# One scan and a reciprocal in place of two scans in a chunked linear-attention kernel

## The chip, the cores and the metric

The kernel runs on one core of a Trainium2 chip. A core has TensorE (PE, matrix products, with a queue of its own for loading weights, PEld), VectorE (DVE), ScalarE (ACT), GpSimd (POOL) and SyncE (SP, which here only issues DMAs). The metric is the device time of one execution in microseconds; the median over the runs counts.

## The reference

The reference is a linear attention with a decay for each channel, followed by a mixture of experts. Batch 4, 8 heads, 768 tokens, head size 48; 8 experts, model width 384, hidden width 1024.

```python
for t in range(S):
    kt, vt, rt, wt = (k[:, :, t], v[:, :, t], r[:, :, t], w[:, :, t])
    cur = np.einsum('bhd,bhe->bhde', u[None] * kt, vt)
    y[:, :, t] = np.einsum('bhd,bhde->bhe', rt, state + cur)
    state = wt[:, :, :, None] * state + np.einsum('bhd,bhe->bhde', kt, vt)
...
skip_score = x @ w_skip
do_compute = skip_score > 0
out = x.copy()
xc = x[do_compute]
e_idx = np.argmax(xc @ w_gate, axis=1)
...
    h = np.maximum(xc[mask] @ w1[e], 0.0)
    y[mask] = gate_w[mask, None] * (h @ w2[e])
out[do_compute] = xc + y
```

The decay `w` lies between 0.8 and 0.95 here. Everything is float32.

## The kernel before

**Chunks.** The 768 tokens of a batch are cut into 6 chunks of 128 tokens, so there are 24 chunks, `i` = 0 to 23. Channels lie on the partitions: two heads of 48 channels at partitions 0 and 64, four such pairs (`NP` = 4) side by side in the free dimension. A tile of one chunk is thus 128 partitions by 4 x 128 numbers. `wrk` holds `w` (4 rows of 129, `CW`, the last column a zero between pairs), `r` and `k` of a chunk.

**What is made of the decays.** `prep_scan` (L277) runs a scan over `w` backwards: `q[j]` is the product of the decays from token `j` to the end of the chunk, started anew at each pair by the `floor` operand, which lies in the PSUM tile `pss`. `prep_keys` takes the reciprocal `rq` of `q[0]`, one number for each pair (L284), forms `kq = k * q[j+1]` on POOL (L287), and runs a second scan, forwards, that gives `rh[j]`, the product of the decays before token `j` (L289). `prep_reads` forms `rp = r * rq * rh` with four operations of DVE, one for each pair (L297), and `rk = r * k` on POOL (L302). `beside` ties POOL's operation to the last of the four `rp`, so that it starts after them. With `kq` and `rp`, PE computes the scores inside a chunk (L328, `psA`), transposes `kq` (L321), and multiplies `rp` with the state (L383).

**The loop.** The order of all work is written out by hand. A pass `s` of the attention loop issues the loads of chunk `s+4`, stores chunk `s-1`, updates and carries the state of chunk `s`, scans chunk `s+2`, forms the outputs of chunk `s` (L378 and L383, into the PSUM tile `psY`), prepares keys and reads of chunk `s+2`, and computes scores, the two masks `asb` (L334) and the bonus (L343, L347) of chunk `s+1`. On DVE the order in a pass is: scan, `rq`, scan, four `rp`, two masks, bonus. The bonus writes `psY`, on which L378 then accumulates. Three `wrk` buffers go round: the load of a chunk waits until POOL's `rk` and ACT's check (L311) of the chunk three before have read theirs. SP issues its DMAs in order.

**The router.** After every sixth chunk a generator `router` computes which expert each token goes to; it yields after each small step, and `drip` issues one, two or four of these steps at fixed places in the pass: before the scan, between `prep_keys` and `prep_reads`, and after the bonus. They run on DVE (shown as L205, a helper's line), some on ACT and POOL, and PE writes its results into `pss`, the same tile in which `floor` lies. Up to two `mark` steps of two ACT operations each come in a pass.

**Weights during attention.** With `k = s - 3`, the first weights are fetched during the attention loop: `load_weights(e, q)` yields after each of three DMAs of 512 KB (L90); `q` = 0 is the first matrix, `q` = 1 the second. They go to two raw buffers: the first matrix of expert 0 to one, the other three in turn to the second. The pass then casts slices of 512 columns to a high part on ACT (`split_slice`, L107); the low part, raw minus high, is put on the list `lows` and taken by POOL in the next pass, beside the scan (L273).

**After attention.** The rest of the router for the last chunks, the first expert's first half on PE meanwhile (L126, L582), then the stage of the experts with gathered tokens (L768 to L795).

Of the kernel before, what the change touches and what calls it, by code (L numbers as in the profile page):

```python
# [8 lines left out]
F32 = mybir.dt.float32  # L9
# [5 lines left out]
ALU = mybir.AluOpType  # L15
# [5 lines left out]
P = 128  # L21
# [5 lines left out]
NP = H // 2  # L27
# [3 lines left out]
CW = P + 1  # L31
# [4 lines left out]
HEAD = 6  # L36
STEP = 214
W_AT = 4
Q_MIN = 1e-30
RW = 1 + NP * CW + 3 * NP * P + 3  # L40
R_OFF = 1 + NP * CW
# [15 lines left out]
def rwkv_moe_kernel(ctx, tc, wrk, wrk0, vN, uP, wgs, wgp, w12, cst, out):  # L57
    nc = tc.nc
# [12 lines left out]
    def beside(ins, op):  # L71
        tc.add_manual_dep(ins.ins, op.ins.name,
                          mybir.DependencyInfo(mybir.DependencyClass.Sync,
                                               mybir.DependencyReason.DATA),
                          reason="shared port")
    WN = ("w1h", "w1l", "w2h", "w2l")

    def wtile(e, k):
        nm = f"{WN[k]}{e % 2}"
        pool = wset0 if nm in ("w1h1", "w1l1", "w2h0", "w2l0") else wset1[0]  # L80
        t = wsp[e, k] = pool.tile([P, KC * DF], F32R, tag=nm, name=f"{nm}_{e}")
        return t
# [11 lines left out]
    def split(dst_h, dst_l, src, eng=None):  # L94
        nc.scalar.copy(dst_h, src)
        (eng or nc.vector).tensor_tensor(dst_l, src, dst_h.bitcast(F32), op=ALU.subtract)

    def split_slice(e, i, eng=None):
        q, cs = i // 6, slice((i % 6) * 512, (i % 6 + 1) * 512)
        for k in (2 * q, 2 * q + 1):  # L100
            if (e, k) not in wsp:
                wtile(e, k)
        hi, lo, raw = wsp[e, 2 * q][:, cs], wsp[e, 2 * q + 1][:, cs], raws[e, q][:, cs]
        if eng is None:
            split(hi, lo, raw)
        else:
            nc.scalar.copy(hi, raw)  # L107
            lows.append((lo, raw, hi.bitcast(F32)))
# [24 lines left out]
    with tc.tile_pool(name="att", bufs=2) as att, \  # L133
# [6 lines left out]
        def load_chunk(i):  # L140
            b, c = seq[i]
            t = wrk_sb[i % NBUF]
            vf = vt_sb[i % (NBUF + 1)].rearrange("p a j -> p (a j)")
            if i == 0:
                nc.sync.dma_start(t[:, :R_OFF], wrk0[:, :R_OFF])
                nc.scalar.dma_start(t[:, K_OFF:V_OFF], wrk0[:, K_OFF:V_OFF])
                nc.sync.dma_start(t[:, R_OFF:K_OFF], wrk0[:, R_OFF:K_OFF])
                nc.scalar.dma_start(c_sb[:, :C_IOTA], cst[:, :C_IOTA])
                nc.sync.dma_start(u_sb, uP)
                nc.scalar.dma_start(vf, wrk0[:, V_OFF:V_OFF + NP * P])  # L150
                return
            for g in range(2):
                nc.sync.dma_start(t[64 * g:64 * g + D], wrk[b, c, g, :, :V_OFF])
            for g in range(2):
                nc.sync.dma_start(vf[64 * g:64 * g + D], wrk[b, c, g, :, V_OFF:V_OFF + NP * P])

        def load_v(i):
            b, c = seq[i]
            v_sb[i] = att.tile([P, H, D], F32, tag="v", name=f"v{i}", bufs=4)
            nc.sync.dma_start(v_sb[i], vN[b, c])  # L160
# [36 lines left out]
        floor = pss[:, 200:200 + NP * CW // 2].bitcast(BF16)  # L197
        pt = pss[:, 64:64 + 2 * NV * E].rearrange("p (j q e) -> p j q e", j=2, q=NV)

        class Steps:  # L200
            last = None
# [9 lines left out]
        def setup():  # L211
# [5 lines left out]
            nc.vector.memset(bias_hi, -Q_MAX)  # L217
            nc.vector.memset(smask, Q_MIN)
            nc.vector.memset(smask[:, :, 0:1], 1.0)
# [32 lines left out]
        def flush():  # L252
            while held:
                held.pop(0)()

        def drip(k=1):
            for _ in range(k):
                while later and next(later[0], None) is None:
                    later.popleft()
# [20 lines left out]

        def prep_keys(i):
            wk = work[i]
            rq = wk["rq"] = att.tile([P, NP, 1], F32, tag="rq", name=f"rq{i}")
            nc.vector.reciprocal(rq, wk["q"][:, :, 0:1])  # L284

            kq = wk["kq"] = att.tile([P, NP, P], F32, tag="kq", name=f"kq{i}")
            nc.gpsimd.tensor_tensor(kq, wk["k"], wk["q"][:, :, 1:CW], op=ALU.mult)  # L287
            rh = wk["rh"] = att.tile([P, NP, CW], F32, tag="rh", name=f"rh{i}", bufs=1)
            nc.vector.tensor_tensor_scan(  # L289
                rh.rearrange("p a j -> p (a j)"), wk["w"][:, 0:NP * CW], floor, 0.0,  # L290
                op0=ALU.mult, op1=ALU.max)

        def prep_reads(i):
            wk = work[i]
            rp = wk["rp"] = att.tile([P, NP, P], F32, tag="rp", name=f"rp{i}", bufs=3)
            for a in range(NP):
                last = nc.vector.scalar_tensor_tensor(  # L297
                    rp[:, a], wk["r"][:, a], wk["rq"][:, a], wk["rh"][:, a, :P],
                    op0=ALU.mult, op1=ALU.mult)

            rk = wk["rk"] = att.tile([P, NP, P], F32, tag="rk", name=f"rk{i}")
            mul = nc.gpsimd.tensor_tensor(rk.rearrange("p a j -> p (a j)"),  # L302
                                          wk["w"][:, R_OFF:K_OFF], wk["w"][:, K_OFF:V_OFF],
                                          op=ALU.mult)
            beside(mul, last)
# [281 lines left out]
        def fill(k):  # L587
            psw = ps1.tile([P, 512], F32, tag="psT", name="psw", bufs=2)
            for _ in range(k):
                nc.tensor.matmul(psw, warm[:, :P], warm, start=True, stop=True)  # L590

        with tc.manual_schedule():
            setup()
            fill(FILL0)
            for s in range(-2, n + 1):
                on = lambda i: 0 <= i < n
                if s + 4 < n:
                    load_chunk(s + 4)
                if on(s + 3) and s + 3 >= 1:
                    load_v(s + 3)  # L600
                if s == -2:
                    nc.sync.dma_start(c_sb[:, C_IOTA:], cst[:, C_IOTA:])
                    nc.sync.dma_start(wgp_sb[:, 0::2], wgp[:, 0::2])
                    nc.sync.dma_start(wgp_sb[:, 1::2, E + 1:], wgp[:, 1::2, :2 * D])
                    nc.sync.dma_start(wgp_sb[:, 1::2, :E + 1], wgp[:, 1::2, 2 * D:])
                if s == -1:
                    nc.sync.dma_start(wgs_sb, wgs)
                if on(s - 1):
                    store(s - 1)
                for i0, m in GROUPS:  # L610
                    if i0 + m == s:
                        pace[0] = 1 if i0 + m < LATE else 2
                        later.append(router(i0, m))
                        if i0 + m == LATE:
                            later.append(early())
                if on(s):
                    update(s)
                    carry(s)
                drip(pace[0])
                if on(s + 2):  # L620
                    prep_scan(s + 2)
                if on(s):
                    outputs(s)
                flush()
                if on(s + 2):
                    prep_keys(s + 2)
                    drip(2 * pace[0])
                    prep_reads(s + 2)
                if on(s):
                    evict(s)  # L630
                if on(s + 1):
                    intra(s + 1)
                    mask(s + 1, 0)
                    mask(s + 1, 1)
                    bonus_sums(s + 1)
                    bonus(s + 1)
                    drip(2 * pace[0])
                if on(s + 2):
                    prep_check(s + 2)
                for _ in range(min(2, len(marks))):  # L640
                    marks.popleft()()
                if s == n - 1:
                    early_tokens(0)
                if on(s):
                    rows_out(s)
                flush()
                if s == -2:
                    nc.vector.tensor_copy(trib, tri)
                    nc.gpsimd.tensor_copy(identb, ident)
                    nc.gpsimd.tensor_copy(iota, c_sb[:, C_IOTA:C_IOTA + 2 * P])  # L650
                k = s + 1 - W_AT
                for eq, k0 in (((0, 1), 0), ((0, 0), 3), ((1, 0), 8), ((1, 1), 16)):
                    if k == k0:
                        gens[eq] = load_weights(*eq)
                    if k0 <= k < k0 + 3:
                        next(gens[eq])
                if 1 <= k < 7:
                    split_slice(0, 5 + k, nc.gpsimd)
                if 9 <= k < 15:
                    split_slice(1, k - 9, nc.gpsimd)  # L660

        while len(later) > 1:
            drip()
# [308 lines left out]
```

## Time and profile before

| | |
|---|---|
| median of 3 runs | 317.33 us (316.35 to 317.79) |
| profiled execution | 317.5 us, of which 315.6 us is the span |
| busy share of the span | PE 93%, PEld 85%, DVE 78%, ACT 59%, POOL 37% |
| scan `q` (L277), 24 times | 29.1 us in all |
| scan `rh` (L289), 24 times | 28.9 us |
| `rp` (L297), 96 times | 33.1 us |
| `kq` and `rk` on POOL, 24 times each | 28.6 and 30.6 us |

The span runs from the first to the last instruction. The attention loop fills about the first half of it; the experts fill the second. Shares are means over both, so the stages have to be looked at by themselves. In rows of the order of time the first number is the start, the second the duration of the group, and brackets hold the idle time of the engine before it and what ended it. Operations of one engine overlap a little at their ends, so that a queue of them advances by somewhat less than the sum of their durations.

### The profile page before, as it was taken

How to read it: one execution, taken by the hardware profiler on the slowest of the kernel's cores; microseconds unless marked ns; L12 is line 12 of the kernel's file. 1: busy time of each engine (PE TensorE's matmuls, PEld its weight loads, DVE VectorE, ACT ScalarE, POOL GpSimd, SP SyncE). 2: the span in 40 equal slices, each digit the busy share in tenths (PEclk: the TensorE clock that was granted, in tenths of full speed). 3: DMA queues.
4: the chain of work that ended last, by engine and by line, in shares of the span. 5: the costliest groups of instructions: out<-in, count | busy, mean ns of one | idle time of the engine just before them, and what ended most of it. 6: DMA issues, size and time to landing. Idle time of an engine off the chain costs nothing.

```text
span 315.6 us, 8456 instructions
## 1 busy us (share of the span) xinstructions
PE 292.2 (93%) x3229; PEld 269.6 (85%) x3229; DVE 244.8 (78%) x505; ACT 185.3 (59%) x527; POOL 115.5 (37%) x118
## 2 busy tenths in 40 slices
PE   7499999899898998979999999999999999999992
PEld 2388888788787887868889899999999999999991
DVE  8899999999999999999637479587785949496310
ACT  4437667689775998766633358274564828184200
POOL 8164455555535566543401772411102020101111
PEclk9879999999999999999999999999999999999998
DMA  7999999999899988885301489756657473630001
GB/s 227 220 214 241 232 292 271 257 264 264 212 233 257 267 187 179 180 206 194 116 25 34 143 294 348 275 195 218 213 199 239 152 256 95 243 143 27 6 4 37
DMA packets 23778, 60.45 MB, mean 192 GB/s; under 512 B 4902, under 2 KB 11338, under 8 KB 23728
## 3 DMA queue, kind: packets, MB, share of 16 engines
q1 hardware_dynamic: 21248, 53.69, 62.6%
q0 software_dynamic: 2048, 5.48, 5.3%
q8 instruction: 27, 0.44, 0.7%
q10 hardware_dynamic: 432, 0.66, 0.6%
q14 instruction: 23, 0.19, 0.2%
HBM read 52.76 MB, written 7.86 MB: 192 GB/s over the span
## 4 chain that ended last, share of the span: by engine, by line
PE 72%; DMA 13%; DVE 10%; POOL 1%; issue 1%; ACT 1%; SPq 0%; POOLq 0%; DVEq 0%
DMA wrk<-wrk 10%; PE psO L790 7%; PE psO L788 7%; PE psO L789 7%; PE psY L378 6%; PE psH L770 6%; PE psH L769 6%; PE psH L768 6%; PE psA L328 6%; PE psY L383 5%; PE psB L343 5%; DVE asb L334 4%; PE psH L126 4%; DVE psY L347 3%; PE psT L321 3%; DVE rp L297 2%
## 5 line engine op out<-in xcount | busy, mean ns | idle before, releaser
L775 ACT ACTIVATE hh<-psH 128x256 fp32r<-128x256 f32 x60 | 23.0, 383 | 56.8 <-PE psH L770 53.5
L732 POOL DMA_INDIRECT out<-fin,ids x16 | 17.0, 1065 | 102.5 <-DVE fin L795 94.7
L770 PE MATMUL psH<-xTh,w1l 128*128 128x256 f32 x168 | 47.6, 283 | 0.0
L769 PE MATMUL psH<-xTl,w1h 128*128 128x256 f32 x168 | 47.6, 283 | 0.0
L768 PE MATMUL psH<-xTh,w1h 128*128 128x256 f32 x168 | 47.6, 283 | 0.0
L302 POOL TENSOR_TENSOR rk<-wrk 128x512 f32<-128x512 f32 x24 | 30.6, 1275 | 28.9 <-DVE rp L297 14.5
L788 PE MATMUL psO<-w2h,hh 128*128 128x384 f32 x120 | 40.8, 340 | 0.0
L790 PE MATMUL psO<-w2h,hl 128*128 128x384 f32 x120 | 40.2, 335 | 0.0
L789 PE MATMUL psO<-w2l,hh 128*128 128x384 f32 x120 | 40.2, 335 | 0.0
L378 PE MATMUL psY<-asb,v 128*48 128x128 f32 x384 | 26.6, 282 | 13.1 <-DVE psY L347 13.0
L287 POOL TENSOR_TENSOR kq<-wrk,q 128x512 f32<-128x512 f32 x24 | 28.6, 1190 | 18.5 <-DVE q L277 13.4
L776 DVE SCALAR_TENSOR_TENSOR hl<-psH,hh 128x256 fp32r<-128x256 f32 x60 | 25.2, 420 | 12.5 <-ACT hh L775 12.1
L334 DVE TENSOR_TENSOR asb<-psA,c_sb 128x512 f32<-128x512 f32 x48 | 30.7, 681 | 4.3 <-PE psA L328 4.3
L378 PEld LDWEIGHTS psY<-asb,v 128*48 128x48 f32 x384 | 20.5, 126 | 15.6 <-DVE psY L347 15.4
L297 DVE SCALAR_TENSOR_TENSOR rp<-wrk,rq,rh 128x128 f32<-128x128 f32 x96 | 33.1, 405 | 0.5
L770 PEld LDWEIGHTS psH<-xTh,w1l 128*128 128x128 f32 x168 | 32.2, 192 | 0.0
L769 PEld LDWEIGHTS psH<-xTl,w1h 128*128 128x128 f32 x168 | 32.2, 192 | 0.0
L768 PEld LDWEIGHTS psH<-xTh,w1h 128*128 128x128 f32 x168 | 32.2, 192 | 0.0
L795 DVE SCALAR_TENSOR_TENSOR fin<-psO,gates,xg 128x384 f32<-128x384 f32 x15 | 9.3, 618 | 28.5 <-PE psO L790 28.5
L289 DVE TENSOR_TENSOR_SCAN rh<-wrk,pss 128x516 f32<-128x516 f32 x24 | 28.9, 1205 | 2.6 <-PE pss L516 1.3
L277 DVE TENSOR_TENSOR_SCAN q<-wrk,pss 128x516 f32<-128x516 f32 x24 | 29.1, 1214 | 1.4 <-DMA wrk<-wrk 1.4
L343 PE MATMUL psB<-rk,ubk_sb 128*128 128x128 f32 x192 | 27.8, 288 | 0.9 <-POOL rk L302 0.9
(145 smaller groups left out, 668.6 us busy)
## 6 DMA issues: line engine op xcount, KB each, us to landing
r<-w SPq DMA_DIRECT2D x48, 512.0 KB, 5.8
wrk<-wrk SPq DMA_DIRECT2D x46, 288.9 KB, 6.3
v<-vN SPq DMA_DIRECT2D x24, 192.0 KB, 6.2
out<-x SPq DMA_DIRECT2D x24, 192.0 KB, 5.4
vt<-wrk SPq DMA_DIRECT2D x46, 96.0 KB, 6.1
wrk<-wrk SPq DMA_DIRECT2D x1, 258.5 KB, 3.8
wrk<-wrk ACTq DMA_DIRECT2D x1, 256.0 KB, 4.0
wrk<-wrk SPq DMA_DIRECT2D x1, 256.0 KB, 4.5
```

Of the source, the lines that this page charges most:

```text
L277: nc.vector.tensor_tensor_scan(q.rearrange("p a j -> p (a j)")[:, ::-1], t[:, 1:1 + NP * CW][:, ::-1], floor, 0.0, op0=ALU.mult, op1=ALU.max)
L297: last = nc.vector.scalar_tensor_tensor(rp[:, a], wk["r"][:, a], wk["rq"][:, a], wk["rh"][:, a, :P], op0=ALU.mult, op1=ALU.mult)
L302: mul = nc.gpsimd.tensor_tensor(rk.rearrange("p a j -> p (a j)"), wk["w"][:, R_OFF:K_OFF], wk["w"][:, K_OFF:V_OFF], op=ALU.mult)
L334: nc.vector.tensor_tensor(s, psa[g], tri.rearrange("p (o j) -> p o j", o=1).to_broadcast([P, NP, P]), op=ALU.mult)
L343: nc.tensor.matmul(wk["psb"][:, a], ubk_sb[:, a], wk["rk"][:, a], start=True, stop=True)
L378: nc.tensor.matmul(psy[64 * g:64 * g + D, a], v[:, 2 * a + g], wk["asb"][g][:, a], start=False, stop=(c == 0), skip_group_check=True)
L768: nc.tensor.matmul(ps, w1h[:, o:o + P], xTh[:, kc], start=(kc == 0), stop=False)
L769: nc.tensor.matmul(ps, w1h[:, o:o + P], xTl[:, kc], start=False, stop=False)
L770: nc.tensor.matmul(ps, w1l[:, o:o + P], xTh[:, kc], start=False, stop=(kc == KC - 1))
L788: nc.tensor.matmul(pso, h[j, fc][0], w2h[:, o], start=(fc == 0), stop=False)
L789: nc.tensor.matmul(pso, h[j, fc][0], w2l[:, o], start=False, stop=False)
L790: nc.tensor.matmul(pso, h[j, fc][1], w2h[:, o], start=False, stop=(fc == FC - 1))
```

## The change

The second scan, `rq` and the four `rp` operations go. In `prep_keys` DVE takes the reciprocal of the whole of `q` (128 x 512) into `rp`; in `prep_reads` one product of 128 x 512 multiplies it with `r` in place. `rk` on POOL stays tied to the last DVE operation of `prep_reads`, now that product. The twelve weight fetches of the attention loop and the slices that are cast are put at other passes: the table `FETCH` names the passes `k` for each of the four matrices.

```diff
+FETCH = (((0, 1), (0, 2, 4)), ((1, 0), (9, 11, 13)), ((0, 0), (10, 12, 14)), ((1, 1), (18, 19, 20)))
...
         def prep_keys(i):
             wk = work[i]
-            rq = wk["rq"] = att.tile([P, NP, 1], F32, tag="rq", name=f"rq{i}")
-            nc.vector.reciprocal(rq, wk["q"][:, :, 0:1])
+
+            rp = wk["rp"] = att.tile([P, NP, P], F32, tag="rp", name=f"rp{i}", bufs=3)
+            nc.vector.reciprocal(rp, wk["q"][:, :, :P])
 
             kq = wk["kq"] = att.tile([P, NP, P], F32, tag="kq", name=f"kq{i}")
             nc.gpsimd.tensor_tensor(kq, wk["k"], wk["q"][:, :, 1:CW], op=ALU.mult)
-            rh = wk["rh"] = att.tile([P, NP, CW], F32, tag="rh", name=f"rh{i}", bufs=1)
-            nc.vector.tensor_tensor_scan(
-                rh.rearrange("p a j -> p (a j)"), wk["w"][:, 0:NP * CW], floor, 0.0,
-                op0=ALU.mult, op1=ALU.max)
 
         def prep_reads(i):
             wk = work[i]
-            rp = wk["rp"] = att.tile([P, NP, P], F32, tag="rp", name=f"rp{i}", bufs=3)
-            for a in range(NP):
-                last = nc.vector.scalar_tensor_tensor(
-                    rp[:, a], wk["r"][:, a], wk["rq"][:, a], wk["rh"][:, a, :P],
-                    op0=ALU.mult, op1=ALU.mult)
+            rp = wk["rp"]
+            last = nc.vector.tensor_tensor(rp, rp, wk["r"], op=ALU.mult)
...
-                for eq, k0 in (((0, 1), 0), ((0, 0), 3), ((1, 0), 8), ((1, 1), 16)):
-                    if k == k0:
+                for eq, at in FETCH:
+                    if k == at[0]:
                         gens[eq] = load_weights(*eq)
-                    if k0 <= k < k0 + 3:
+                    if k in at:
                         next(gens[eq])
-                if 1 <= k < 7:
-                    split_slice(0, 5 + k, nc.gpsimd)
-                if 9 <= k < 15:
-                    split_slice(1, k - 9, nc.gpsimd)
+                if 2 <= k < 8:
+                    split_slice(0, 4 + k, nc.gpsimd)
+                if 11 <= k < 17:
+                    split_slice(1, k - 11, nc.gpsimd)
```

## The prediction

> **What bounds the kernel now.** I read the views from coarse to fine: busy time by stretches, then who waited for whom, then the order of time on each engine. A pass `s` of the attention loop is called slot `s`; I date it from its first `psY` matmul (L378) to that of slot `s+1`. First stretches of 10 us: start:end, then busy us of PE, PEld, DVE, ACT and POOL, the granted clock, the DMA share and GB/s. Then the summed waits, and the chain that ended last (start, us, what).
>
> ```profile
> 20.00:30.00 10.00, 10.00 (x157) 8.92 (x154) 9.61 (x19) 6.12 (x24) 4.17 (x5) 1.00 1.05 227
> 40.00:50.00 10.00, 9.95 (x157) 8.72 (x156) 9.86 (x21) 7.02 (x23) 5.28 (x5) 1.00 1.05 279
> 70.00:80.00 10.00, 9.62 (x165) 8.29 (x163) 9.86 (x16) 9.61 (x32) 5.52 (x6) 1.00 1.02 266
> PE psY L378 <- DVE psY L347: 13.0, 15, 4.1
> 28.86 0.88 PE psY L378 x16
> 34.74 0.88 PE psY L378 x16
> 57.55 1.08 PE psY L378 x16
> ```
>
> PE and DVE are both nearly full, so a share of busy time doesn't tell which sets the pace. The waits do: PE stops for DVE in front of one group only, 15 times, 13.0 us in all. Slots 2 to 5 have no such stop and last 5.88 us (28.86 to 34.74): there PE sets the pace, and a faster DVE is worth nothing. The chain also shows that this group adds 0.88 us to a PE that runs on, but 1.08 after a stop; a stop that goes is worth its idle time and 0.2 more. Next the stops themselves (start, us, the group, idle time before it).
>
> ```profile
> 16.05 1.95 PE L378 MATMUL psY<-asb,v 128*48 128x128 f32 x16 [4.08 <-DVE psY L347]
> 57.55 1.08 PE L378 MATMUL psY<-asb,v 128*48 128x128 f32 x16 [0.90 <-DVE psY L347]
> 76.87 1.08 PE L378 MATMUL psY<-asb,v 128*48 128x128 f32 x16 [0.38 <-DVE psY L347]
> 83.42 1.08 PE L378 MATMUL psY<-asb,v 128*48 128x128 f32 x16 [0.99 <-DVE psY L347]
> 96.08 1.08 PE L378 MATMUL psY<-asb,v 128*48 128x128 f32 x16 [0.75 <-DVE psY L347]
> 115.39 1.08 PE L378 MATMUL psY<-asb,v 128*48 128x128 f32 x16 [0.37 <-DVE psY L347]
> 121.96 1.08 PE L378 MATMUL psY<-asb,v 128*48 128x128 f32 x16 [0.99 <-DVE psY L347]
> 135.58 1.08 PE L378 MATMUL psY<-asb,v 128*48 128x128 f32 x16 [1.49 <-DVE psY L347]
> 155.75 1.08 PE L378 MATMUL psY<-asb,v 128*48 128x128 f32 x16 [0.51 <-DVE psY L347]
> ```
>
> One stop is the start (4.08). The other 14, from 57.55 to 155.75, hold 13.0 - 4.1 = 8.9 us. They lie in the slots where the router's small operations are dripped between DVE's large ones. Four of them (76.87, 83.42, 115.39, 121.96: 2.73 us) stand where ACT is full too (9.61 of 10 in 70 to 80). The other ten hold 6.15.
>
> **One slot of DVE and POOL.** Its order on DVE is scan `q`, `rq`, scan `rh`, four `rp`, two masks `asb`, the bonus `psY` that releases PE.
>
> ```profile
> 28.27 1.22 DVE L277 TENSOR_TENSOR_SCAN q<-wrk,pss 128x516 f32<-128x516 f32 x1
> 29.52 0.18 DVE L284 RECIPROCAL rq<-q 128x4 f32<-128x4 f32 x1
> 29.62 1.20 DVE L289 TENSOR_TENSOR_SCAN rh<-wrk,pss 128x516 f32<-128x516 f32 x1
> 29.62 1.18 POOL L287 TENSOR_TENSOR kq<-wrk,q 128x512 f32<-128x512 f32 x1 [1.99 <-DVE q L277]
> 30.85 1.14 DVE L297 SCALAR_TENSOR_TENSOR rp<-wrk,rq,rh 128x128 f32<-128x128 f32 x4
> 32.35 1.29 DVE L334 TENSOR_TENSOR asb<-psA,c_sb 128x512 f32<-128x512 f32 x2 [0.35 <-PE psA L328]
> 33.55 0.69 DVE L347 TENSOR_TENSOR psY<-psB,vt 128x512 f32<-128x512 f32 x1
> ```
>
> From the start of scan `q`: `rq` at 1.25, `rh` at 1.35, `rp` at 2.58, done for the queue at 3.63 (1.14 less the 0.09 by which the next operation starts ahead of a result); masks 1.20 and bonus 0.60 follow, 5.43 in all. POOL's `kq` runs from 1.35 to 2.53, just under `rh`.
>
> **What the new operations cost.** Groups by shape: count | busy us, mean ns | idle time before, by releaser; the L297 row gives min/median/max.
>
> ```profile
> L289 DVE TENSOR_TENSOR_SCAN rh<-wrk,pss 128x516 f32<-128x516 f32 x24 | 28.9, 1205 | 2.6 <-PE pss L516 1.3 <-PE pss L446 0.9 <-ACT tab L523 0.4
> L347 DVE TENSOR_TENSOR psY<-psB,vt 128x512 f32<-128x512 f32 x24 | 16.5, 687 | 0.0
> L205 DVE TENSOR_TENSOR dl<-lg,mx 128x48 f32<-128x48 f32 x4 | 0.8, 208 | 0.0
> L205 DVE TENSOR_SCALAR sm<-sm 128x6 f32<-128x6 f32 x4 | 0.7, 172 | 0.1
> L284 DVE RECIPROCAL rq<-q 128x4 f32<-128x4 f32 x24 | 4.3, 179 | 0.8
> L205 DVE RECIPROCAL gate<-sm x4: 164/182/191, 64.2 to 167.0; 128x6 f32<-128x6 f32 x4
> L220 DVE CAST smaskb<-smask 128x516 bf16<-128x516 f32 x1 | 0.6, 561 | 0.0
> L297 DVE SCALAR_TENSOR_TENSOR rp<-wrk,rq,rh x96: 329/346/1267, 7.8 to 153.1; 128x128 f32<-128x128 f32 x96
> 71.87 1.28 POOL L273 TENSOR_TENSOR w2l<-r,w2h 128x512 fp32r<-128x512 f32 x1 [0.30 <-ACT w2h L107]
> 72.84 2.17 DVE L297 SCALAR_TENSOR_TENSOR rp<-wrk,rq,rh 128x128 f32<-128x128 f32 x4
> 73.11 1.23 POOL L287 TENSOR_TENSOR kq<-wrk,q 128x512 f32<-128x512 f32 x1
> ```
>
> The 128x512 reciprocal is the price that this trace doesn't show. A two-input operation grows by (687 - 208)/(512 - 48) = 1.03 ns for each element. Reciprocals of 4 and 6 elements take 179 and 182 ns (median), one of 6 took 164, less than the 172 of a TENSOR_SCALAR of 6. At 1.03 ns the large one would take 179 + 508 x 1.03 = 700 ns. Lower end: the cast of 516 elements, 0.56 us. Upper end: the slowest reciprocal of 6 is 19 ns over the TENSOR_SCALAR, 3.2 ns an element more, so 4.2 ns and 2.1 us for 512. I take 0.70, because 4 and 6 elements differ by about 1.5 ns each and not by 4. In the queue an operation of 687 ns takes a step of 0.60 (two masks from 32.35 to 33.55 above), so this one takes 0.62.
>
> [...]
>
> The product `rp * r` has two inputs in SBUF, as the old `rp` had. The rows of 71.87 to 75.01 show what that costs beside POOL: four `rp` take 2.17 instead of 1.14 us, one of them up to 1267 ns, because they get the port only between POOL's `w2l` and `kq` and after them. So the product, ready at 1.25 + 0.62 = 1.87, waits for the end of `kq` at 2.53 and is done at 3.13, against 3.63 now. Queued behind it are masks and bonus, and behind those PE. An ordinary slot gains 0.50 us on DVE, not the 1.2 that the operations' times say (4.93 instead of 5.43). Router operations between reciprocal and product lie in that wait, so two of them are free. The stalls of `rh` on `pss` (2.6 us in the L289 row) go with it, as the reciprocal reads `q` alone. Where `kq` comes late, behind `w2l`, the product waits for `w2l` alone and passes ahead of `kq`, as the first `rp` did; `kq` then comes 0.6 later, and its reader on PE a slot later still has it in time. POOL's `rk`, tied to the last `rp`, comes 0.5 earlier, and with it the release of `wrk` for SP's next load.
>
> **What it is worth, stop by stop.** What is late next is PE itself, so each of the ten stops is worth at most its idle time and 0.2: 6.15 + 2.0 = 8.15. In three of them DVE stays last, since those slots (6, 12, 18; the first chunk of a batch has no L383) are PE's short ones:
>
> ```profile
> 53.28 1.18 POOL L287 TENSOR_TENSOR kq<-wrk,q 128x512 f32<-128x512 f32 x1
> 91.76 1.18 POOL L287 TENSOR_TENSOR kq<-wrk,q 128x512 f32<-128x512 f32 x1 [1.98 <-DVE q L277]
> 129.24 1.22 DVE L277 TENSOR_TENSOR_SCAN q<-wrk,pss 128x516 f32<-128x516 f32 x1
> 64.41 0.21 ACT L463 CAST vals<-gate 128x6 bf16<-128x6 f32 x1 [2.52 <-DVE gate L205]
> r<-w SPq DMA_DIRECT2D x12, 512.0 KB, 7.5
> q1 hardware_dynamic: 15920, 34.62, 86.4%
> ```
>
> - Slot 6: `kq` ends at 54.46; product, masks, bonus (0.60 + 1.20 + 0.69) and 0.05 to release give 57.00 for 57.55: 0.55 of a possible 1.10.
> - Slot 12: `kq` ends at 92.94, hence 95.48 for 96.08: 0.60 of 0.95.
> - Slot 18: scan at 129.24, reciprocal done at 131.12, four router operations 0.9, product 132.6, bonus 134.5: 1.05 of 1.69.
>
> That takes 1.55 away: 6.6 us. The four stops of ACT's full slots hold 2.73 + 0.8 = 3.5. There ACT works without a pause from 64.41 on, so its next `psY` copy can't come sooner than its own work lets it; between 0 and 3.5 I take 1.4, nearer to 0 because ACT is 96% busy in 70 to 80 and only in the last of each set does DVE alone hold PE (0.99). At the start, masks can come 1.1 earlier, but `kq` of chunk 1 is held on POOL and PE needs it next: 0.35, between 0 and 1.1.
>
> The weight fetches move 6.3 MB of the 34.62 on that queue to other slots: the same 12 issues of 512 KB on SP. Pieces land 7.5 us after their issue; in the new order their first cast comes two slots (11.8) later, so ACT's queue gets no wait for them. ACT's casts (0.61) and POOL's low halves (1.27) move one slot later for one matrix and two for the other; POOL's part is covered by scan `q`, ACT's by its idle time outside 64 to 84. Without that cover one cast is 0.6 a slot, in slot 10 alone of the crowded ones. I count 0, between -1 and +1. After 166 us nothing that the change touches is left but the last pieces, which the expert stage reads; the rest moves forward unchanged.
>
> Sum: 6.6 + 1.4 + 0.35 = 8.35. The profiled execution took 317.5 (span 315.6), 0.2 over the median 317.33. 317.5 - 8.35 = 309.15; on the median 309.0.
>
> **Rivals.**
> 1. Slower: the reciprocal has a higher price per element. Up to a step of 1.28 it hides under `kq`; at 1.78 a slot is as long as now (1.25 + 1.78 + 0.60 = 3.63); beyond, DVE sets every slot. [...] For it: no large reciprocal is in the trace. Against it: 164 and 182 ns. Chance 0.10.
> 2. Most of the gain is not seen: if the reciprocal keeps `kq` off the port, `kq` ends at 1.25 + 0.62 + 1.2 = 3.1 and the product at 3.7, as now; only the 2.6 us of `pss` stalls goes: 315. For it: DVE and POOL do exclude each other above. Against it: the scan, with one input in SBUF, runs beside `kq` at full speed. [...] Chance 0.11.
> 3. DMA becomes the bound: slots 12 to 17 now carry six pieces in a row, 10.2 MB; at the 266 to 279 GB/s of the rows above that is 37 to 38 us, when PE needs six times 5.88, 35.3. Chunks are loaded two slots ahead, so the lag of 2 mostly fits; if not, 311 to 312. Chance 0.09.
>
> **The numbers.** Forecast 0.70, with its own range 306.5 to 312.5: the ACT term from 0 to 3.5, the start from 0 to 1.1, fetches 1 either way, and the ten stops up to 1.5 more. Rivals 0.10, 0.11, 0.09. A change under 0.5% (1.6 us) can't be told from none. Faster: forecast, rival 3 and two thirds of rival 2, 0.86; same 0.04; slower 0.10. The range 305.8 to 315.8 takes in rivals 2 and 3 and leaves out rival 1 and the far ends.
>
> **What would show it.** RECIPROCAL 128x512 near 0.70 us; the product's TENSOR_TENSOR stretched to about 1.2 where it waits for `kq`; no DVE wait on `pss` in that place; PE's waits at L378 down from 13.0 to about 6, start included; slots of PE near 5.9 in 57 to 150; ACT still full in slots 8 to 10. A reciprocal above 1.8 us, `kq` starting only after the reciprocal, or DVE waiting for `wrk` around slots 14 to 17 would make it wrong.

## The result, and the profile after

The changed kernel takes 343.36 us (343.13 to 343.93) beside 317.56 for the kernel before: 1.0821 of it, with a 95% interval of 1.0786 to 1.0856. It is slower by 26 us, where 309.0 with a range of 305.8 to 315.8 was forecast. The profiled execution took 343.36, its span is 341.6 against 315.6. In the later sets of runs the kernel before itself took 327 to 328 us, and the traces of those sets, all of other kernels, show 9 to 12 us more behind the attention loop but the same 5.88 us for a slot that PE sets, so comparisons there are by ratio to the runs beside them, or by the loop alone.

The span splits at the first and the last start of a `psY` group, L378 before and L373 after. The start moved from 16.05 to 17.96 (+1.9), the loop from there to the last group grew from 144.9 to 168.9 (+23.9), the rest is 154.6 and 154.8. The loss lies in the loop and its start alone.

DVE's order of time in the changed kernel, one slot and the head of the next:

```profile
31.91 1.22 DVE L278 TENSOR_TENSOR_SCAN q<-wrk,pss 128x516 f32<-128x516 f32 x1
33.16 3.35 DVE L286 RECIPROCAL rp<-q 128x512 f32<-128x512 f32 x1
36.55 0.69 DVE L294 TENSOR_TENSOR rp<-rp,wrk 128x512 f32<-128x512 f32 x1
37.16 1.28 DVE L329 TENSOR_TENSOR asb<-psA,c_sb 128x512 f32<-128x512 f32 x2
38.36 0.69 DVE L342 TENSOR_TENSOR psY<-psB,vt 128x512 f32<-128x512 f32 x1
38.95 1.22 DVE L278 TENSOR_TENSOR_SCAN q<-wrk,pss 128x516 f32<-128x516 f32 x1
```

From scan to scan 7.04 us, without a gap: 1.25, the reciprocal's step of 3.39, 0.61 for the product, 1.20, 0.59. PE has 5.88 us of work for such a slot and now waits for the rest: the stops of 0.96 below and the 0.2 that a stop adds make up the 1.16 between the two. From the changed kernel's view of waits (us in all, times, the longest), its view of groups, and PE's order of time:

```profile
PE psY L373 <- DVE psY L342: 31.0, 21, 3.1
```

```profile
L286 DVE RECIPROCAL rp<-q 128x512 f32<-128x512 f32 x24 | 80.5, 3353 | 0.8
```

```profile
39.10 1.08 PE L373 MATMUL psY<-asb,v 128*48 128x128 f32 x16 [0.96 <-DVE psY L342]
46.14 1.08 PE L373 MATMUL psY<-asb,v 128*48 128x128 f32 x16 [0.96 <-DVE psY L342]
```

The stops of PE in front of this group went from 13.0 to 31.0 us, the larger part of the loss. The 24 reciprocals take 80.5 us and the products 16.5; the second scan, `rq` and the four `rp` in whose place they stand took 28.9 + 4.3 + 33.1 = 66.3. DVE is busy for 163.6 of the 169 us from 18 to 187, so it sets the pace. One thing went as reckoned: the 2.6 us that the second scan lost to `pss` are gone; the 0.8 in the reciprocal's row is not put down to `pss`.

The theory was then that the price of the 128x512 reciprocal is the whole of the loss, and that the rest of the prediction holds. The rivals: that the fetches take part, or that the order of the operations and DVE and POOL excluding each other do.

### The profile page after: what moved, and what is told of

Its sections match the earlier page's. It is cut to its first block, busy times and chain, and to the rows that moved or that the text cites. A ratio compares the mean times of both kernels' runs of the same rounds, so it can differ in the third digit from the quotient of the medians.

```text
span 341.6 us, 8363 instructions
## 1 busy us (share of the span) xinstructions
PE 296.8 (87%) x3229; PEld 273.5 (80%) x3229; DVE 276.0 (81%) x409; ACT 185.5 (54%) x527; POOL 116.4 (34%) x118
## 4 chain that ended last, share of the span: by engine, by line
PE 48%; DVE 26%; DMA 14%; issue 6%; POOL 2%; SPq 1%; POOLq 0%; DVEq 0%; ACT 0%
DVE rp L286 11%; DMA vt<-wrk 7%; DVE asb L329 6%; PE psO L783 6%; PE psO L785 6%; PE psO L784 6%; DMA wrk<-wrk 6%; PE psH L765 6%; PE psH L764 6%; PE psH L763 6%; DVE q L278 4%; DVE psY L342 3%; PE psY L378 2%; PE psY L373 2%; POOL rk L297 2%
## 5 line engine op out<-in xcount | busy, mean ns | idle before, releaser
L286 DVE RECIPROCAL rp<-q 128x512 f32<-128x512 f32 x24 | 80.5, 3353 | 0.8
L373 PE MATMUL psY<-asb,v 128*48 128x128 f32 x384 | 27.8, 290 | 31.1 <-DVE psY L342 31.0
L373 PEld LDWEIGHTS psY<-asb,v 128*48 128x48 f32 x384 | 21.2, 129 | 34.2 <-DVE psY L342 34.0
L771 DVE SCALAR_TENSOR_TENSOR hl<-psH,hh 128x256 fp32r<-128x256 f32 x60 | 25.2, 420 | 12.5 <-ACT hh L770 12.1
L383 ACT COPY xT<-psY 128x512 f32<-128x512 f32 x24 | 14.0, 585 | 30.5 <-PE psY L378 26.8
L338 PE MATMUL psB<-rk,ubk_sb 128*128 128x128 f32 x192 | 28.7, 294 | 0.3 <-POOL rk L297 0.3
```

The costliest lines, as they stand in the source:

```text
L286: nc.vector.reciprocal(rp, wk["q"][:, :, :P])
L338: nc.tensor.matmul(wk["psb"][:, a], ubk_sb[:, a], wk["rk"][:, a], start=True, stop=True)
L373: nc.tensor.matmul(psy[64 * g:64 * g + D, a], v[:, 2 * a + g], wk["asb"][g][:, a], start=False, stop=(c == 0), skip_group_check=True)
```

## The experiments

**The price by itself.** A row of reciprocals on DVE in the setup of the kernel before; the added work changes the start, so only the durations count.

```diff
+            for n_ in (1, 2, 4, 6, 8, 16, 32, 64, 128, 256, 512):
+                nc.vector.reciprocal(pro[:, :n_], prb[:, :n_])
+                nc.vector.tensor_tensor(pro[:, :n_], prb[:, :n_], prb[:, :n_], op=ALU.mult)
...
+            for n_ in (6, 12, 24):
+                nc.vector.tensor_tensor(pro[:, :n_], prb[:, :n_], prb[:, :n_], op=ALU.mult)
+                nc.vector.reciprocal(pro[:, :n_], pro[:, :n_])
...
+                nc.vector.memset(prs, 1.5)
+                nc.vector.reciprocal(pro[:, :n_], prb[:, :n_])
```

> The kernel before with a row of reciprocals of 1 to 512 elements added to DVE's setup, each followed by a product of the same size, and some of 6, 12 and 24 elements behind a product that they need, or behind a memset they don't. The added work changes the time of the start, so only the durations are read. If the price is a constant per element: a straight line through 179 ns at 4 and 3353 ns at 512 elements, 6.25 ns each over 154 ns, so 191 ns at 6 and 954 at 128. If there is a cheap form for few elements: 4 to 16 elements near 180 ns and the line only above. The reciprocals of 6 in the trace before (164 to 191 ns) would be explained if the one behind a long memset is shorter than the one behind the product it needs.

Groups by shape in this kernel (count | busy us, mean ns). L230 is the first loop, L236 the reciprocal behind the product it needs, L239 the one behind a memset that it doesn't need:

```profile
L230 DVE RECIPROCAL pro<-prb 128x512 f32<-128x512 f32 x1 | 3.4, 3353 | 0.0
L230 DVE RECIPROCAL pro<-prb 128x256 f32<-128x256 f32 x1 | 1.8, 1753 | 0.0
L230 DVE RECIPROCAL pro<-prb 128x128 f32<-128x128 f32 x1 | 1.0, 953 | 0.0
L230 DVE RECIPROCAL pro<-prb 128x16 f32<-128x16 f32 x1 | 0.3, 253 | 0.0
L230 DVE RECIPROCAL pro<-prb 128x6 f32<-128x6 f32 x1 | 0.2, 191 | 0.0
L230 DVE RECIPROCAL pro<-prb 128x4 f32<-128x4 f32 x1 | 0.2, 178 | 0.0
L236 DVE RECIPROCAL pro<-pro 128x6 f32<-128x6 f32 x1 | 0.2, 191 | 0.0
L239 DVE RECIPROCAL pro<-prb 128x6 f32<-128x6 f32 x1 | 0.1, 131 | 0.0
L231 DVE TENSOR_TENSOR pro<-prb 128x6 f32<-128x6 f32 x1 | 0.2, 166 | 0.0
```

One line from 4 to 512 elements: 153 ns and 6.25 ns for each. There is no cheap form for few. And the same 6 elements take 191 ns behind an operation on the same tile and 131 behind a memset of 516 elements that has nothing to do with them: 60 ns of the fixed part disappear there, and 58 and 57 at 12 and 24 elements (227 and 303 against 169 and 246). Something like it, though smaller, was in the trace before. Of its four reciprocals of 6, the one of 164 ns stood behind a scan that it doesn't need, the one of 191 behind its producer `sm`:

```profile
137.19 1.20 DVE L289 TENSOR_TENSOR_SCAN rh<-wrk,pss 128x516 f32<-128x516 f32 x1
138.31 0.16 DVE L205 RECIPROCAL gate<-sm 128x6 f32<-128x6 f32 x1
166.76 0.17 DVE L205 TENSOR_SCALAR sm<-sm 128x6 f32<-128x6 f32 x1
166.97 0.19 DVE L205 RECIPROCAL gate<-sm 128x6 f32<-128x6 f32 x1
```

Whether the shortening comes from not depending on the operation ahead, or from that operation being long, no run separates.

**The fetches apart from the arithmetic.** Two kernels: the new arithmetic with the old `FETCH` order, and the old arithmetic with the new one. Of the first:

```diff
-                for eq, at in FETCH:
-                    if k == at[0]:
+                for eq, k0 in (((0, 1), 0), ((0, 0), 3), ((1, 0), 8), ((1, 1), 16)):
+                    if k == k0:
...
-                if 2 <= k < 8:
-                    split_slice(0, 4 + k, nc.gpsimd)
+                if 1 <= k < 7:
+                    split_slice(0, 5 + k, nc.gpsimd)
```

The second is the fetch part of the change alone on the kernel before.

> The reciprocal and the product as changed, the weight fetches and casts at their old passes. Theory A (the 3.35 us of the large reciprocal on DVE are the whole loss, the fetches are neutral): 343, within 1.5. Theory B (the fetches at their new passes, six in a row in slots 12 to 17, take part in the loss): 340 or less. Theory C (the new passes of the fetches save time under the longer slots): 345 or more.

> The kernel before with only the weight fetches and casts moved to their new passes. Theory A: 317.5, within 1.5, since PE, DVE and POOL have the same work in the same order but for casts one or two slots later. Theory B: 319 or more. Theory C: 316 or less.

Measured: 344.02 us, 1.0833 of before (1.0787 to 1.0878), for the first; 316.85, 0.9983 (0.9966 to 1.0000), for the second. The loop of the second is 145.2 us against 144.9. The fetches are neutral within what can be told; theories B and C fall in both runs.

**The reciprocal taken out.** In the changed kernel, with everything else kept:

```diff
-            nc.vector.reciprocal(rp, wk["q"][:, :, :P])
+            nc.vector.memset(rp, 1.0)
```

> The changed kernel with the 128x512 reciprocal replaced by a memset of the same 128x512 tile (about 0.49 us, as the memsets of 128x512 in the trace before); the reciprocal itself is left out. All else of the change stays: product behind kq, no second scan, new fetches. Theory A, with the rest of the prediction right: 309.0, between 306.5 and 312.5, PE stopping about 6 us in front of the psY group. Rival (the order or the shared port costs more than reckoned, whatever the reciprocal's price): 314 or more.

Measured: 310.85 us (310.14 to 312.75), 0.9775 of before (0.9741 to 0.9810), inside the range that was given for it. DVE's and POOL's order in a slot without router work, and PE's waits, in this kernel:

```profile
29.43 1.22 DVE L278 TENSOR_TENSOR_SCAN q<-wrk,pss 128x516 f32<-128x516 f32 x1
30.70 0.48 DVE L286 MEMSET rp<- 128x512 f32 x1
30.78 1.17 POOL L289 TENSOR_TENSOR kq<-wrk,q 128x512 f32<-128x512 f32 x1 [2.79 <-DVE q L278]
31.22 1.28 DVE L294 TENSOR_TENSOR rp<-rp,wrk 128x512 f32<-128x512 f32 x1
33.50 1.29 DVE L329 TENSOR_TENSOR asb<-psA,c_sb 128x512 f32<-128x512 f32 x2 [1.00 <-PE psA L323]
```

```profile
PE psY L373 <- DVE psY L342: 6.4, 6, 3.9
```

This is the slot that the prediction described. The product, ready at 31.22, takes 1.28 us instead of 0.69, as `kq` on POOL ends at 31.95 only; then DVE waits 1.00 us for PE, so PE sets the pace. Of 13.0 us of stops 6.4 are left, 3.9 of them the start. With 0.48 us in the reciprocal's place the change is worth 2.3%. Behind the loop this kernel takes 154.8 us, as long as the kernel before (154.6), so the values that are left out don't change the experts' time.

The profiled execution is the longest of the four, and shows what comes next. ACT's copy into `x` waits for an earlier store, POOL's `vals` stands behind it, and DVE behind that:

```profile
138.43 0.54 ACT L403 COPY x<-psX 128x192 f32<-128x192 f32 x2 [2.19 <-DMA out<-x]
141.06 0.21 POOL L496 TENSOR_TENSOR vals<-gd,vals 128x6 bf16<-128x6 f32 x1 [2.14 <-ACT vals L493]
141.30 0.41 DVE L206 TENSOR_TENSOR sg<-oh,vals 128x240 bf16<-128x240 bf16 x1 [3.14 <-POOL vals L496]
```

That slot, 20, takes 8.59 us instead of 6.90. It comes behind the slots 12 to 17 that fetch weights in a row. The same kernel with the old fetch order was to show whether they cause it.

> As memset_for_recip (the reciprocal is left out), but with the weight fetches and casts at their old passes. That run stood at 0.9775 of the kernel before, and its trace has ACT waiting for the store of x to land and DVE waiting 3.1 us behind it in slot 20, after six slots with a fetch each. If those fetches in a row are what is missing to the forecast (rival 3 of the prediction): 0.970 to 0.975 here. If DMA is as late with the old passes, or the fetches are worth nothing once DVE is short: 0.977 to 0.980.

Measured: 321.01 us against 327.23 for the kernel before, whose runs there spread from 321.5 to 328.8, so there is no interval and the expectation is not decided. In its trace the loop takes 139.3 us against 141.0, ACT never waits for a store, DVE waits 0.98 us instead of 3.14 at that place, and slot 20 takes 6.22. With the new order ACT had waited for stores three times, 5.0 us in all. But three of the four executions of that kernel were 1.5 to 2.6 us shorter than the profiled one, by themselves as much as the difference, and four other traces with the new order (the fetches alone, and the faster version below three times) have no such wait. So one execution shows the lateness of DMA, and it isn't settled whether the order of the fetches brings it about.

**Half a reciprocal.** Two of the four pairs by reciprocal, a memset for the other two, which are left out:

```diff
-            nc.vector.reciprocal(rp, wk["q"][:, :, :P])
+            nc.vector.reciprocal(rp[:, :2], wk["q"][:, :2, :P])
+            nc.vector.memset(rp[:, 2:], 1.0)
```

> The changed kernel with the reciprocal of two of the four pairs (128x256) and a memset in place of the other two, which are left out. By the line measured before, the reciprocal takes 1.75 us; with the memset's 0.25 the step in DVE's queue is 2.0, a slot 1.25 + 2.0 + 0.61 + 1.8 = 5.7: just under PE's 5.88 where no router work is dripped, and over it where there is. Price theory: 318, between 316 and 322, about the kernel before, as the break-even of the prediction (1.78) says. If the loss doesn't go by the length of the reciprocal but comes with a full-size one: near 311 or near 343.

Measured: 327.18 us, 0.9976 of the runs beside it (0.9955 to 0.9998), about the same as before, as the price theory has it. The expectation's 316 to 322 us was for a kernel before of 317; as a ratio it is 0.995 to 1.014. Of this kernel, a slot of DVE:

```profile
29.37 1.22 DVE L278 TENSOR_TENSOR_SCAN q<-wrk,pss 128x516 f32<-128x516 f32 x1
30.62 1.75 DVE L286 RECIPROCAL rp<-q 128x256 f32<-128x256 f32 x1
32.38 0.27 DVE L287 MEMSET rp<- 128x256 f32 x1
32.69 0.69 DVE L295 TENSOR_TENSOR rp<-rp,wrk 128x512 f32<-128x512 f32 x1
```

The step from 30.62 to 32.69 is 2.07. The prediction had put the break-even of DVE's work at 1.78 for a slot without router work. Such slots stay at 5.88 us here, as PE sets them; over the whole loop the break-even lies a little above 2.07 (144.1 against 144.9). The stalls on `pss`, 2.6 us in the kernel before, are gone besides and may make the difference; no run takes them apart.

**A fill of the same length.** To see whether anything but the length counts, DVE does other work in the reciprocal's place, which is left out. First six memsets of 128x512 and one of 128x128 into `rp`; then one of 128x512 and a long one into a spare tile:

```diff
-            nc.vector.reciprocal(rp, wk["q"][:, :, :P])
+            nc.vector.memset(rp, 1.0)
+            nc.vector.memset(spare, 1.0)
```

> The changed kernel with six memsets of 128x512 and one of 128x128 on DVE in place of the reciprocal, which is left out: about 3.3 us of DVE in the same place. Price theory (only the length on DVE's queue counts): 343, within 3. Rival (the reciprocal also does something to POOL, to the port or to the clock): 338 or less.

> The reciprocal left out; in its place two memsets of DVE that don't wait for each other, one of 128x512 into the same tile and one of 128x3000 bf16 into a spare tile, 3.1 to 3.6 us together. If only the length on DVE's queue counts, a slot without router work lasts 1.28 + length + 0.61 + 1.20 + 0.60, and the time is that of the changed kernel (1.082 of before) plus or minus 22 slots times the difference of the lengths: 1.06 to 1.10. If the reciprocal does something beyond its length: 1.04 or less for the same slot length.

Measured: 372.5 us, 1.1333 (1.1303 to 1.1364), for the first, a miss against its expectation; 355.47, 1.0953 (1.0714 to 1.1192), for the second, whose interval is wide, as the runs of the kernel before beside it spread from 321.5 to 328.8. DVE's order shows why the first missed. First rows of the six memsets, then rows of the long fill:

```profile
35.81 0.48 DVE L287 MEMSET rp<- 128x512 f32 x1
36.47 0.48 DVE L287 MEMSET rp<- 128x512 f32 x1 [0.17 <-DVE rp L287]
39.88 0.69 DVE L296 TENSOR_TENSOR rp<-rp,wrk 128x512 f32<-128x512 f32 x1
```

```profile
33.85 0.48 DVE L287 MEMSET rp<- 128x512 f32 x1
34.91 2.56 DVE L288 MEMSET spare<- 128x3000 bf16 x1 [0.57 <-DVE rp L287]
37.38 0.63 DVE L296 TENSOR_TENSOR rp<-rp,wrk 128x512 f32<-128x512 f32 x1
```

The memsets into one tile stand 0.17 us apart, so the first fill takes a step of 4.07 and not 3.3. The second was meant to have no wait, but there DVE idles 0.57 us ahead of the memset into the other tile; why is open. Its step is 3.53, the reciprocal's 3.39. Slots without router work last 7.75, 7.14 and 7.04 us: 3.68, 3.61 and 3.65 beyond the step. The loops are 186.1, 172.4 and 168.9. To within 0.07 us a slot goes by the length on DVE's queue, whatever fills it.

**A version that is faster than before.** Keep the second scan, but start it from the reciprocal of `q[0]`, pair by pair, so that one product replaces the four `rp`:

```diff
+            nc.vector.reciprocal(rp[:, :, 0:1], wk["q"][:, :, 0:1])
...
+            for a in range(NP):
+                nc.vector.tensor_tensor_scan(
+                    rp[:, a, 1:], wk["w"][:, 1 + a * CW:P + a * CW], floor[:, 1:P], rp[:, a, 0:1],
+                    op0=ALU.mult, op1=ALU.max)
...
+            last = nc.vector.tensor_tensor(rp, rp, wk["r"], op=ALU.mult)
```

> The kernel before, with the reciprocal of q[0] (4 elements) written to the first column of rp, four scans of 127 elements that start from it in place of the scan over 516, and one product of 128x512 in place of four rp operations; old fetches. If four short scans take about 1.35 us of the queue (4 x 0.33) and the product 0.60, the stretch from scan q to the masks is 2.05 instead of 2.38, and each of the 14 stops loses up to 0.33: 313.5, between 312 and 316. If a scan that starts from a value just written waits for it, or short scans have a large fixed part (0.5 us each): 317 to 322.

> The same with the weight fetches and casts at their new passes. If the fetches are worth what they were alone (0.9983 of the kernel before): 0.5 us less than four_scans. If they matter more once DVE holds PE less: 1 us less or better; if six fetches in a row make DMA late: 1 us more.

> The same kernel as four_scans_new_fetch, beside another run of the kernel before: 0.986 to 0.994, as the first gave 0.9914 (0.9886 to 0.9941). If that gain hung on the state of that chip: 0.995 or more.

> The kernel of four_scans_new_fetch once more, since the runs beside its second one were disturbed. 0.986 to 0.994 of the kernel before, and an attention loop (first to last start of a psY group) of 142 to 143.6 us instead of 144.9, as in the two traces so far. If the gain is not real: 0.996 or more and a loop of 144.5 or more.

Measured: 0.9926 (0.9905 to 0.9948) with the old fetches; with the new ones 0.9914 (0.9886 to 0.9941), then 1.0063 (0.9963 to 1.0163), outside what was expected, then 0.9910 (0.9887 to 0.9933). The 1.0063 goes by the two shortest of eleven runs of the kernel before; against their median, 327.23, its 325.87 is 0.996. The loops of the three traces with new fetches are 142.4, 143.5 and 142.4 against 144.9. The one that is longer has it all in slot 0: 7.76 us at a granted clock of 0.61, where the third has 6.76 at 0.75; PE's groups `psA` and `psB` take 1.97 and 1.74 us there, 1.52 and 1.16 in the third. From the second group on the three loops are 135.8, 135.7 and 135.7 us long, that with old fetches 135.9, the kernel before 138.2. So the gain is 0.7 to 0.9%, less than the 1.2% in the middle of what was expected, and not for the reason expected. The short scans have a step of 0.40 each, not 0.33, and a slot's DVE work without router operations is as long as before (3.69 to the masks against 3.63). Most of the gain lies in slots 10 and 16, which fall from 6.55 to 5.69 and from 6.57 to 5.70 us; with the new fetches slot 15 gives 0.5 more. DVE and POOL in slot 10, first in the kernel before, then in the last of these runs:

```profile
78.43 1.27 POOL L273 TENSOR_TENSOR w2l<-r,w2h 128x512 fp32r<-128x512 f32 x1 [2.00 <-DMA wrk<-wrk]
79.31 2.26 DVE L297 SCALAR_TENSOR_TENSOR rp<-wrk,rq,rh 128x128 f32<-128x128 f32 x4
79.66 1.23 POOL L287 TENSOR_TENSOR kq<-wrk,q 128x512 f32<-128x512 f32 x1
```

```profile
78.26 1.58 DVE L290 TENSOR_TENSOR_SCAN rp<-wrk,rp,pss 128x127 f32<-128x127 f32 x4
79.88 0.69 DVE L297 TENSOR_TENSOR rp<-rp,wrk 128x512 f32<-128x512 f32 x1
79.92 1.70 POOL L288 TENSOR_TENSOR kq<-wrk,q 128x512 f32<-128x512 f32 x1
80.49 1.28 DVE L332 TENSOR_TENSOR asb<-psA,c_sb 128x512 f32<-128x512 f32 x2
```

The single product comes first and `kq` waits for it (1.70 instead of 1.18); four `rp` had let `kq` in after the first of them and taken 2.26. That the product passes ahead of a late `kq` is what the prediction said. It hangs on who starts first: in slot 9 of the same run `kq` starts at 73.35 and the product at 73.44, the product takes 1.64, and the slot lasts 6.44 us, as long as before (6.47).

## Why the prediction was wrong

**The step that failed** is the price of the 128x512 reciprocal, in "What the new operations cost": 0.70 us with an upper end of 2.1, where 3.353 was measured. It is a term that was mis-sized by 4.8 times, and its upper end was too low as well. The working took the 164 ns of a reciprocal of 6 elements as proof that an element costs little. That one stood behind a scan that it doesn't depend on and was 27 ns shorter than the one behind its producer, more than the 12.5 that two elements more than `rq` cost; in the row of reciprocals that was measured by itself, the one behind a memset was 60 ns shorter. The upper end compared the 191 ns with a TENSOR_SCALAR and not with the reciprocal of 4. Rows nearer to the answer were in the trace: 178 to 181 ns at 4 elements, 191 at 6, both behind their producers, hence 5 to 6.5 ns an element and 2.7 to 3.5 us for 512. Taking the median over reciprocals in different company hid that.

**Rival 1 was right** in mechanism: far above its break-even of 1.78, DVE sets the pace. A slot without router work, 1.25 + step + 0.60 + 1.8 for masks and bonus, gives 7.04 with the measured step of 3.39, and 7.04 was measured. The 22 slots from 16.05 to 155.75, 139.7 us in the kernel before, would by that take 154.9, and the kernel 333; measured were 163.6 for these slots, as those with router work, which this sum leaves out, last up to 8.3, and 1.9 more for the start. Its chance of 0.10 was too low for a price that no row of the trace showed.

**What held** once the reciprocal is out of the way. The sum was 309.0; with the memset 310.85 was measured. The product waiting for `kq` (1.28 us), PE as the next bound, PE's stops down to about 6 us (6.4), the three slots where DVE stays last (stops of 0.34, 0.24 and 0.86 are left in front of 58.13, 93.72 and 129.62), the stalls on `pss` gone, the fetches counted at zero: each is in the traces. Term by term the agreement is looser, and that the sum comes so near is in part luck. In the profiled execution, whose span is 4.6 us shorter than before, the four slots of ACT's stops gain 2.7 where 1.4 was reckoned. Nine of the ten others gain 4.5 where 5.9 was: slot 21, counted at 0.7, gains nothing, as a stop of 0.51 stays in front of 151.01, and slot 18 gains 0.6 where 1.05 was reckoned. The tenth, slot 20, gets 1.7 longer with the late store; rival 3 had seen the danger of late DMA, though in other slots. The start, reckoned as a gain of 0.35, loses 1.15: the first group comes 0.8 sooner, but slot 0 lasts 8.73 us instead of 6.76, with a stop of 1.08 for `kq` of chunk 1 and a granted clock of 0.61 instead of 0.71 (`psA` and `psB` on PE take 1.97 and 1.90 us instead of 1.55 and 1.16). Rival 2 fell: `kq` starts 0.1 us after the reciprocal does, 33.26 after 33.16 in the changed kernel, and runs at its full speed:

```profile
33.26 1.18 POOL L289 TENSOR_TENSOR kq<-wrk,q 128x512 f32<-128x512 f32 x1 [1.62 <-PE psY L373]
```

That DVE's products and POOL's exclude each other is in the rows, 2.17 us for four `rp` instead of 1.14 in the kernel before and 1.28 for the one product instead of 0.69 with the memset. That it is a port they contend for is the author's reading; no row shows what keeps them apart.

## What to carry to other kernels

A price per element is read from two sizes of the same operation in the same company, both behind the operation that makes their input; one short duration behind unrelated work proves little (131 ns there for 6 elements, 191 behind their producer). Where the whole change hangs on one operation that the trace shows only for a few elements, that operation deserves most of the doubt, and a break-even price worked out beforehand tells what the doubt is worth. Where operations of two engines exclude each other, as DVE's products and POOL's do here, one long operation can pass ahead of the other engine's next one where four short ones let it in between: in slot 10 `kq` took 1.70 us behind the one product, and 1.23 among four `rp` that took 2.26.

## What the hardware showed that was not expected

A reciprocal on DVE costs 6.25 ns for each element of a partition over a fixed 153, six times the 1.03 ns of an element of a two-input product, at every size from 4 to 512. A reciprocal of 6 elements is 60 ns shorter behind an unrelated memset of 516 (131 against 191). Memsets of DVE into the same tile stand 0.17 us apart, and 0.57 us of idle time lie between one into `rp` and one into another tile. A scan of 127 elements takes a step of 0.40 us, so four of them take 1.62 where one of 516 took 1.23. Between executions of one and the same kernel, slot 0 lasted 7.76 us at a granted clock of 0.61, and 6.54 and 6.76 at 0.74 and 0.75.
